# Block 0's Q moved behind its G, block 1 turned in squares on VectorE, seven-product Q on blocks 1 and 2: an adaLN linear-attention block

## The chip, the cores and the metric

The kernel runs on one core of one Trainium2 chip. The metric is the device time of one execution in microseconds (us), the median of several runs. TensorE is called PE here, VectorE DVE, ScalarE ACT, GpSimd POOL, and SyncE, which only issues DMAs, SP.

## What is computed

x is 2048 x 512, in float32; c is a conditioning vector of 512. The reference, cut to what matters:

```python
mod = (silu(c) @ w_mod).reshape(1, 6, 1, 512)        # sa, ca, ga, sb, cb, gb
h = layernorm(x) * (1 + ca) + sa
q, k, v = split of (h @ wqkv) into 32 heads of 16
pq, pk = phi(q), phi(k)                              # phi(t) = where(t > 0, t + 1, exp(t)) + 1e-6
kv  = einsum("bhsd,bhse->bhde", pk, v);  z = sum of pk over s
o   = einsum("bhqd,bhde->bhqe", pq, kv) / (einsum("bhqd,bhd->bhq", pq, z) + 1e-6)
x   = x + ga * (o @ wo)
h   = layernorm(x) * (1 + cb) + sb
x   = x + gb * (mish(h @ w1 + b1) @ w2)              # w1: 512 x 1792, w2: 1792 x 512
```

## The kernel before

The 2048 rows are four blocks of 512 rows (b = 0 to 3), and each block is four tiles of 128 rows (t) or, after it is turned, four tiles of 128 columns of D (j or k). Every product of float32 is made of three products of half-exact parts: `split` writes a tensor as a high part (a copy rounded to float32r, suffix h) and a low part (the rest, suffix l, by DVE), and `mm3` adds high x high, high x low and low x high on PE. So in front of each matmul group stand a copy on ACT or POOL and a subtraction on DVE.

The stages in the order of the program, as PE sees them:

- Modulation: `mod_col(i)` multiplies one 128-row piece of w_mod's transpose with silu(c) on DVE and sums it into a column of `mc`. The 24 columns come in groups of four; 0 to 7 are needed first, 8 to 11 are ga, 12 to 19 the second norm's, 20 to 23 gb. `mod_side` loads and makes them a few at a time beside other work.
- For each block: layer norm statistics and the apply (`ln_side`, `ln_begin`), turning the block so that D lies on the partitions, scale and shift by `mc` into `hf`, and `split` into `hT`. Blocks 0 and 1 are turned by PE (sixteen 128 x 128 transposes each; for block 1 in `transpose`, line 279). Blocks 2 and 3 are turned by DVE in 32 x 32 squares (`turn`, line 239), whose result sixteen DMAs of 64 KB carry to their places (`move_squares`, line 256: eight issued by SP, eight by POOL); ACT then reads them (`scale_turned`, line 270).
- K of the block (`k_unit`): products into PSUM, then `k_post`: two ACT passes (exp and relu), one DVE operation to `ku`, the split to `pk`; POOL adds `ku` into a running sum with an accumulating DMA. G of the block (`g_unit`): x's split normed rows times `pk`, added over all blocks in four PSUM banks `gacc`. kv is later made from G, without making V.
- The sums z of `pk` (`z_unit`, `z_side`), which scale the mask `hmask`.
- Q. For blocks 0 and 1 together with seven products of half size instead of eight (`q_sevens`, with sums of quarters prepared by `q_left` and `q_right`), for blocks 2 and 3 plainly (`q_unit`). `beside_q(n)` runs other work at seven places within. `phi` makes each Q tile in two ACT passes and one DVE operation.
- For each block `attend`: den, sixteen small products of Q with `hmask`, its reciprocal, a round trip through DRAM that spreads it over the partitions (`rden_d`, `rd`), Q times `rd`, and the split to `qs`. Then O (`o_unit`), Q times the product of kv and wo. Some O banks are seeded with x by an ACT copy ahead (`o_seed`, in the order of the list SEEDS), and an O tile's end is an ACT pass with a sum, further passes for the second norm (`norm_first`), and turns.
- The second half (w1, mish, w2), which takes the most time and which the change does not touch.

The order on each engine is the order in which the program emits its instructions, and each engine runs its queue in that order. Side work is a Python generator: `spawn` hands one over, and each `tick()` advances all by one `yield`. SBUF tiles come from 93 slots; PSUM from eight banks, four of tag `acc`, three `h`, one `tp`, each given to the next tile once all readers of the last are done.

`make_constants` (line 151 on) makes, on POOL, the constant `w32` and two masks of the block diagonal, `bmask` and `hmask`; DVE reduces `bmask` to `kvmask`. Before, it stands ahead of block 0's third G.

Of the kernel before, what the change touches and what calls it, by code (L numbers as in the profile page):

```python
# [10 lines left out]
AF = mybir.ActivationFunctionType  # L11
# [14 lines left out]
def block_kernel(ctx: ExitStack, tc: tile.TileContext, x, wqkv, wo, w1, b1t, w2, c, wmodt, out):  # L26
# [94 lines left out]
    for j in range(4):  # L121
        load_x(1, j)
    b1c = cst.tile([P, NF], F32, name="b1c")
# [150 lines left out]
    def transpose(key, b, j, sc0, sh0, ptag, hi_engine=act):  # L274

        if b < 2:
            p = ps(ptag, f"tp_{key}_{b}_{j}")
            for t in range(4):
                pe.transpose(p[:, P * t:P * (t + 1)], xt[key, b, t][:, P * j:P * (j + 1)], ident)

        def post():
            hf = sb(f"hf_{key}_{b}_{j}")
            if b < 2:
                hfx[b, j] = hf
                act.activation(hf, p, AF.Identity, bias=mc[:, sh0 + j:sh0 + j + 1],
                               scale=mc[:, sc0 + j:sc0 + j + 1])
            else:
                scale_turned(key, b, j, hf, sc0, sh0)
            yield from split(f"hT_{key}_{b}_{j}", hf, hT, (key, b, j), hi_engine=hi_engine)

        return post()
# [102 lines left out]
    def q_right(c):  # L394

        b11, b12, b21, b22 = [hfx.pop((b, k)) for k in (c, c + 2) for b in (0, 1)]
# [8 lines left out]
    def q_product(o, left, right, tag=None, onto=None):  # L405

        p = onto if onto is not None else ps(tag, f"pq_{left}_{o}")
        for c in range(2):
# [5 lines left out]
            mv_ = qb[right, c] if right[0] == "t" else hT["x", int(right[2]) - 1, c + 2 * (right[1] == "2")]  # L414
# [6 lines left out]
    def q_sevens(side):  # L421
# [21 lines left out]
        for o in range(2):  # L443
            q_product(o, "a12", "b21", onto=p11[o])
            result(0, o, p11[o], None)
# [8 lines left out]
        for o in range(2):  # L454
            result(0, 2 + o, q_product(o, "a22", "t4", onto=pa[o]), None)
        result(1, 2, pc[0], u3[0])
        side(4)
        pc[1] = q_product(1, "s1", "t1", "acc")
        result(1, 3, pc[1], u3[1])
        side(5)  # L460
        for o in range(2):
            q_product(o, "s4", "b22", onto=pc[o])
            result(1, o, pc[o], u2[o])
# [138 lines left out]
    for k in range(4):  # L602
        hi, lo = sb(f"hT_x_0_{k}h", F32R), sb(f"hT_x_0_{k}l", F32R)
        hT["x", 0, k] = hi, lo
        hf_k = hfx[0, k] = sb(f"hf_x_0_{k}")
# [125 lines left out]
    def z_side():  # L731
# [12 lines left out]
        yield  # L744
        for k in range(4):
# [952 lines left out]
```

## Time and profile before

| what | value |
|---|---|
| three runs | 477.77, 478.94, 479.31 us |
| their median | 478.94 us |
| span of the profiled execution | 476.5 us |
| PE busy | 470.8 us (99%) |
| DVE busy | 389.4 us (82%) |
| ACT busy | 312.0 us (65%) |
| POOL busy | 138.7 us (29%) |
| granted TensorE clock | 1.000 |

The span is the time from the first to the last instruction of the one execution that was profiled; the median of the runs is 2.4 us above it. Busy time counts an engine's instructions; register, branch and DMA-issuing instructions are not counted, except those that POOL issues. In a row of the order in time stand the start, the time that the row covers, the engine, the line, the operation, what is written and read, how many instructions, and in brackets the idle time ahead with what ended it. An instruction's time overlaps that of the next by a little, so the distance of two starts is what one costs on its queue.

### The profile page before, as it was taken

What the parts mean: (1) busy time and instruction counts of PE and PEld (TensorE: products, weight loads), DVE (VectorE), ACT (ScalarE), POOL (GpSimd) and SP (SyncE); (2) the same over time, 40 slices, a digit from 0 to 9 for tenths busy, and PEclk for the clock granted to TensorE, in tenths of its full rate; (3) what the DMA queues carried; (4) which work ended last, traced back from release to release, by engine and by line L of the source; (5) the groups of instructions that cost most, each with busy time, mean ns of one, the idle gap of its engine ahead of it and who ended that gap; (6) DMA issues with size and microseconds to landing.
All of it is one profiled execution on the core that took longest, in us unless ns stands there. A gap on an engine that the chain in (4) does not pass through costs nothing.

```text
span 476.5 us, 7242 instructions
## 1 busy us (share of the span) xinstructions
PE 470.8 (99%) x2354; PEld 387.6 (81%) x2354; DVE 389.4 (82%) x783; ACT 312.0 (65%) x566; POOL 138.7 (29%) x236
## 2 busy tenths in 40 slices
PE   8999999999999999999999999999999999999997
PEld 6778888878877888888888888888888888888887
DVE  6989898998998889697979863898544897779992
ACT  6976659756777976688688756694255676637700
POOL 3576261100023255012235325343011101354400
PEclk9999999999999999999999999999999999999999
DMA  8903649743685346936548669999633603498974
GB/s 302 383 22 74 126 93 268 187 144 105 229 213 147 115 119 184 319 119 196 178 153 243 201 187 324 366 308 261 202 96 89 132 2 89 110 221 163 239 157 106
DMA packets 81568, 85.44 MB, mean 179 GB/s; under 512 B 23505, under 2 KB 55769, under 8 KB 81530
## 3 DMA queue, kind: packets, MB, share of 16 engines
q1 hardware_dynamic: 55176, 47.08, 33.6%
q0 software_dynamic: 24096, 37.12, 29.6%
q10 hardware_dynamic: 2258, 0.79, 0.7%
q8 instruction: 18, 0.29, 0.2%
q14 instruction: 20, 0.16, 0.1%
HBM read 55.32 MB, written 22.81 MB: 164 GB/s over the span
## 4 chain that ended last, share of the span: by engine, by line
PE 93%; DVE 2%; ACT 2%; POOL 1%; DMA 1%; issue 0%; ACTq 0%
PE p_a L1265 15%; PE o L1004 9%; PE p_s L1265 8%; PE oacc L75 5%; PE oacc L74 5%; PE oacc L76 5%; PE m L74 5%; PE m L76 5%; PE m L75 5%; PE pk L319 5%; PE p L1265 4%; PE gacc L357 3%; PE gacc L359 2%; PE gacc L353 2%; PE pk L322 2%; PE pq_a L417 2%
## 5 line engine op out<-in xcount | busy, mean ns | idle before, releaser
L843 POOL DMA_DIRECT2D wb<-w2d x14 | 9.8, 705 | 65.1 <-PE p L1265 29.6
L1270 DVE TENSOR_TENSOR cb<-p_s,u 128x512 f32<-128x512 f32 x28 | 19.1, 685 | 11.8 <-ACT u L1319 10.2
L1257 ACT ACTIVATE ub<-cb,b1c 128x512 f32<-128x512 f32 x28 | 20.0, 719 | 9.4 <-DVE cb L1270 9.1
L199 POOL TENSOR_TENSOR rs_n<-rs_n,half 128x1 f32<-128x1 f32 x16 | 10.1, 630 | 38.8 <-DVE rs_n L225 18.7
L1594 POOL DMA_DIRECT2D wt_m<-w2t x20 | 14.0, 702 | 25.2 <-PE m L76 16.9
L1275 ACT ACTIVATE p<-p_a 128x512 f32<-128x512 f32 x12 | 7.0, 582 | 19.5 <-PE p_a L1265 11.7
L1319 ACT ACTIVATE u<-p_a 128x512 f32<-128x512 f32 x14 | 8.4, 597 | 13.6 <-PE p_a L1265 13.4
L1232 ACT ACTIVATE u<-p,b1c 128x512 f32<-128x512 f32 x14 | 9.6, 684 | 11.5 <-PE p L1265 11.5
L1232 ACT ACTIVATE u<-p_a,b1c 128x512 f32<-128x512 f32 x14 | 9.6, 686 | 8.5 <-PE p_a L1265 8.3
L849 POOL DMA_DIRECT2D w2b<-w2d x20 | 10.6, 541 | 12.9 <-PE oacc L76 6.8
L313 POOL DMA_DIRECT2D ku<-ku x10 | 8.9, 1036 | 18.5 <-DVE ku L304 18.3
L270 ACT ACTIVATE hf_n<-sq_n,mc 128x512 f32<-128x512 f32 x16 | 12.0, 802 | 2.4 <-DMA sq_n<-wide_n 2.4
L304 DVE SCALAR_TENSOR_TENSOR q<-e_q,relu_q 128x512 f32<-128x512 f32 x16 | 10.9, 687 | 1.6 <-ACT relu_q L302 1.6
L199 POOL TENSOR_TENSOR rs_x<-rs_x,half 128x1 f32<-128x1 f32 (+1 forms) x10 | 7.8, 785 | 13.8 <-DVE rs_x L194 13.0
L304 DVE SCALAR_TENSOR_TENSOR ku<-e_k,relu_k 128x512 f32<-128x512 f32 x16 | 10.9, 681 | 0.9 <-ACT relu_k L302 0.9
L190 DVE BATCH_NORM_STATS2 st_x<-x 128x6 f32<-128x512 f32 x13 | 8.8, 676 | 3.1 <-DMA x<-in_x_dram 3.1
L966 DVE SCALAR_TENSOR_TENSOR q<-q,rd 128x512 f32<-128x512 f32 x16 | 10.4, 684 | 1.2 <-DMA rd<-rden_d 1.2
L256 POOL DMA_DIRECT2D sq_n<-wide_n x16 | 8.7, 553 | 6.8 <-DMA rd<-rden_d 6.8
L175 DVE SCALAR_TENSOR_TENSOR wm<-wm,sc_row 128x512 f32<-128x512 f32 x16 | 10.5, 682 | 0.0
L256 POOL DMA_DIRECT2D sq_x<-wide_x x16 | 8.9, 566 | 5.1 <-DVE wide_x L239 4.6
L301 ACT ACTIVATE e_k<-pk 128x512 f32<-128x512 f32 x16 | 9.5, 591 | 1.4 <-PE pk L322 1.4
L208 ACT ACTIVATE x<-x,nb_x,rs_x 128x512 f32<-128x512 f32 x9 | 7.1, 809 | 4.8 <-DVE nb_x L203 3.9
(1638 smaller groups left out, 1857.1 us busy)
## 6 DMA issues: line engine op xcount, KB each, us to landing
wm<-in_wmodt_dram SPq DMA_DIRECT2D x24, 256.0 KB
w1p<-in_w_dram SPq DMA_DIRECT2D x24, 256.0 KB
w2b<-w2d POOLq DMA_DIRECT2D x20, 256.0 KB, 7.4
wt_m<-w2t POOLq DMA_DIRECT2D x20, 256.0 KB, 3.7
r<-in_x_dram SPq DMA_DIRECT2D x16, 256.0 KB
x<-in_x_dram SPq DMA_DIRECT2D x15, 256.0 KB
w2r<-in_w_dram SPq DMA_DIRECT2D x14, 256.0 KB
wb<-w2d POOLq DMA_DIRECT2D x14, 256.0 KB, 3.5
```

Source lines behind the costliest of these rows:

```text
L74: pe.matmul(o, st[0], mv[0], start=start, stop=False)
L75: pe.matmul(o, st[0], mv[1], start=False, stop=False)
L76: pe.matmul(o, st[1], mv[0], start=False, stop=stop)
L199: pool.tensor_tensor(y, y, half[:, lo:hi], op=ALU.pow)
L256: queues[n % len(queues)].dma_start(v[32 * m:32 * (m + 1), :, a, :], w[32 * a:32 * (a + 1), m:16:4].rearrange("p j t c -> p j (t c)"))
L304: dve.scalar_tensor_tensor(dst, e, 1.0, r, op0=ALU.min, op1=ALU.add)
L319: pe.matmul(p[t], hT["x", b, k][0][:, P * t:P * (t + 1)], wk[k][n], start=k == 0 and n == 0, stop=False)
L1004: pe.matmul(p, qs[b, g][l][:, ts], ms[g][r], start=not seeded and (g, l, r) == (0, 0, 0), stop=(g, l) == (3, 1), skip_group_check=seeded)
L1232: act.activation(u, p, AF.Mish, bias=b1c[:, f:f + 1])
L1257: act.activation(u, p, AF.Mish, bias=b1c[:, f:f + 1])
L1265: pe.matmul(p, st, mv, start=onto is None and c == 0 and i == 0, stop=c == 1 and i == 2, skip_group_check=onto is not None)
L1270: dve.tensor_tensor(out, p, u, op=ALU.add)
```

## The change

It leaves the products as they are, but for sixteen transposes, and moves work:

- Block 1 is turned as blocks 2 and 3 are: `transpose` becomes `normed`, without PE; four `turn` on DVE and one `move_squares` (eight DMAs from SP, eight from POOL) are added for it.
- Q of block 0 is made plainly, in two pairs of products (`q_pair`), right behind block 0's G. For that the Q weights are loaded early, ahead of x of blocks 2 and 3, and split early, half of the copies on POOL.
- `q_sevens` works on blocks 1 and 2 (MIDDLE), so `q_right` takes `hf` of these, and only block 3 has `q_unit`. All four O tiles of block 0 then follow Q of block 3 at once, and those of block 1 behind them.
- den of block 0 is made within `q_sevens`, den of the others earlier too; the last part of `z_side` moves up for it.
- `make_constants` moves behind the `ln_turn` of block 2.
- Columns 20 to 23 and 16 to 19 of the modulation move from `q_sevens` to the stretch behind block 1's K; columns 12 to 15 take their place.

```diff
@@ loads at the start
     for j in range(4):
         load_x(1, j)
+    for k in range(4):
+        load_wqkv(0, k)
+    for b in (2, 3):
+        for j in range(4):
+            load_x(b, j)
     b1c = cst.tile([P, NF], F32, name="b1c")
...
-    def transpose(key, b, j, sc0, sh0, ptag, hi_engine=act):
-
-        if b < 2:
-            p = ps(ptag, f"tp_{key}_{b}_{j}")
-            for t in range(4):
-                pe.transpose(p[:, P * t:P * (t + 1)], xt[key, b, t][:, P * j:P * (j + 1)], ident)
...
+    MIDDLE = 1, 2
+
+    def normed(key, b, j, sc0, sh0, hi_engine=act):
+
+        hf = sb(f"hf_{key}_{b}_{j}")
+        if b in MIDDLE:
+            hfx[b, j] = hf
+        scale_turned(key, b, j, hf, sc0, sh0)
+        yield from split(f"hT_{key}_{b}_{j}", hf, hT, (key, b, j), hi_engine=hi_engine)
...
@@ behind block 0's K
     step(kpost[3])
+    turn("x", 1, 0, xt["x", 1, 0])
     sums_shift("x", 1, 3, sums3)
     apply(1, 3, act, shift=False)
-    step(xsplit[3], kpost[3])
-    make_constants()
-    for b in (2, 3):
-        for j in range(4):
-            load_x(b, j)
+    wq_halves = [split(f"wq_{k}", wraw[0, k], wq, k, hi_engine=act if k % 2 else pool) for k in range(4)]
+    step(*wq_halves, xsplit[3], kpost[3])
+    for t in (1, 2, 3):
+        turn("x", 1, t, xt["x", 1, t])
+    move_squares("x", 1, (sp, pool))
+    for w in wq_halves:
+        run(w)
     g_unit(0, 2)
     spawn(ln_side(2))
     spawn(mod_side(range(8, 12), 2, 6))
     tick()
+    g_unit(0, 3)
+    tick()
+
+    def q_pair(b, two):
+
+        p = {g: ps("h", f"pq_{b}_{g}") for g in two}
+        for l, r in (0, 0), (0, 1), (1, 0):
+            for k in range(4):
+                for g in two:
+                    pe.matmul(p[g], wq[k][l][:, P * g:P * (g + 1)], hT["x", b, k][r],
+                              start=(l, r, k) == (0, 0, 0), stop=(l, r, k) == (1, 0, 3))
+        for g in two:
+            pq[b, g] = sb(f"q_{b}_{g}")
+            spawn(phi(p[g], f"q_{b}_{g}", pq[b, g]))
+
+    q_pair(0, (0, 1))
+    spawn(ln_begin(2))
+    tick()
     for j in range(4):
-        tr = transpose("x", 1, j, 4, 0, "h" if j < 3 else "tp", pool)
-        step(tr)
+        tr = normed("x", 1, j, 4, 0, pool if j % 2 else act)
+        next(tr)
         spawn(tr)
-    g_unit(0, 3)
-    spawn(ln_begin(2))
+    q_pair(0, (2, 3))
     spawn(ln_turn(2, (0, 1), ()))
     tick()
+    make_constants()
...
@@ blocks 1 to 3
         if b + 2 < NB:
             spawn(ln_side(b + 2))
+            spawn(mod_side([20, 21, 22, 23, 16, 17, 18, 19], 2))
...
-    SEEDS = [(0, 0), (0, 1), (0, 2), (0, 3), (), (), (1, 0), (1, 1), (), (), (), (2, 2)]
+    SEEDS = [(0, 0), (0, 1), (0, 2), (0, 3), (), (1, 0), (1, 1), (), (), (2, 2)]
...
@@ beside_q
+        if n == 2:
+            attending.append(attend(0, 3))
+            next(attending[0])
+            spawn(attending[0])
         if n == 4:
-            spawn(mod_side([20, 21, 22, 23, 16, 17, 18, 19], 2))
+            spawn(mod_side(range(12, 16), 1))
...
@@ behind q_sevens
     for g in range(4):
-        q_unit(2, g)
-        if g == 1:
-            spawn(attending)
+        if g == 3:
+            seed_next()
+        q_unit(3, g)
+        if g == 0:
+            spawn(attend(1, 4))
         if g == 2:
-            spawn(attend(1, 4))
-        if g == 1:
-            spawn(mod_side(range(12, 16), 1))
+            spawn(attend(2, 5, sp))
...
-    for g in range(4):
+    seed_next()
+    spawn_idle(early_rows[1])
+    for t in range(4):
         seed_next()
-        q_unit(3, g)
+        o_unit(0, t)
+        spawn(norm_first(0, t))
         tick()
...
```

Three places of the order that this makes. First POOL's queue behind its last cast for block 0 (`pk_0_3h`), before; `w32`, `bmask` and `hmask` are the constants, `hT_x_1_*` block 1's turned tiles:

```order
L84 CAST pk_0_3h_419<-ku_0_3_346 128x512
L153 MEMSET w32_139 128x128
L155 MEMSET bmask_427 128x128
L157 AFFINE_SELECT bmask_427<-bmask_427 128x128
L159 AFFINE_SELECT bmask_427<-bmask_427 128x128
L163 MEMSET hmask_140 128x128
```

and now, from the same cast on; `sq_x_1` and `sq_x_2` are the squares of blocks 1 and 2:

```order
L84 CAST pk_0_3h_443<-ku_0_3_370 128x512
L84 CAST wq_0h_450<-wr_0_0_111 128x512
L84 CAST wq_2h_456<-wr_0_2_115 128x512
L261 DMA sq_x_1_467<-wide_x_1_446 32x4x128 x8
L204 TENSOR_TENSOR rs_x_2_501<-rs_x_2_501,half_137 128x4
L84 CAST hT_x_1_1h_583<-hf_x_1_1_581 128x512
L84 CAST hT_x_1_3h_593<-hf_x_1_3_591 128x512
L261 DMA sq_x_2_645<-wide_x_2_640 32x4x128 x8
L158 MEMSET w32_163 128x128
L160 MEMSET bmask_663 128x128
L162 AFFINE_SELECT bmask_663<-bmask_663 128x128
L164 AFFINE_SELECT bmask_663<-bmask_663 128x128
```

The constants moved behind sixteen DMA issues, eight for each of the two blocks. Second, DVE's queue around the last turn of block 2 (`wide_x_2`), before; `ku_1_0` belongs to block 1's K:

```order
L239 STREAM_TRANSPOSE wide_x_2_549<-x_2_1_437 128x16x32
L304 SCALAR_TENSOR_TENSOR ku_1_0_587<-e_k_1_0_588,relu_k_1_0_589 128x512
L88 TENSOR_TENSOR xn_1_0l_593<-x_1_0_103,xn_1_0h_592 128x512
L90 SCALAR_TENSOR_TENSOR pk_1_0l_610<-ku_1_0_587,pk_1_0h_609 128x512
L304 SCALAR_TENSOR_TENSOR ku_1_1_613<-e_k_1_1_614,relu_k_1_1_615 128x512
```

and now; `wm_8` and `wm_9` are two `mod_col`:

```order
L244 STREAM_TRANSPOSE wide_x_2_640<-x_2_1_121 128x16x32
L166 TENSOR_REDUCE kvmask_165<-bmask_663 128x32
L300 SCALAR_TENSOR_TENSOR q_0_2_622<-e_q_0_2_630,relu_q_0_2_631 128x512
L300 SCALAR_TENSOR_TENSOR q_0_3_623<-e_q_0_3_634,relu_q_0_3_635 128x512
L300 SCALAR_TENSOR_TENSOR ku_1_0_689<-e_k_1_0_690,relu_k_1_0_691 128x512
L88 TENSOR_TENSOR xn_1_0l_695<-x_1_0_103,xn_1_0h_694 128x512
L180 SCALAR_TENSOR_TENSOR wm_8_509,mc_166<-wm_8_509,sc_row_167 128x512
L180 SCALAR_TENSOR_TENSOR wm_9_511,mc_166<-wm_9_511,sc_row_167 128x512
L90 SCALAR_TENSOR_TENSOR pk_1_0l_712<-ku_1_0_689,pk_1_0h_711 128x512
```

Between the turn and `ku_1_0` now stand the reduction of the mask, which stood far ahead, and two tiles of block 0's Q. Third, PE within `q_sevens`, where one of the seven products ends for the second column half and the next begins for the first; `pq_a11_1` and `pq_a11_0` are the banks of the two halves. Before:

```order
L417 MATMUL pq_a11_1_1313<-qt_0_1h_941,qs12_0l_1111 128x512
L417 MATMUL pq_a11_1_1313<-qt_1_1h_1019,qs12_1h_1169 128x512
L417 MATMUL pq_a11_1_1313<-qt_1_1l_1020,qs12_1h_1169 128x512
L417 MATMUL pq_a11_1_1313<-qt_1_1h_1019,qs12_1l_1170 128x512
L417 MATMUL pq_a11_0_1304<-qt_0_2h_978,qs34_0h_1127 128x512
L417 MATMUL pq_a11_0_1304<-qt_0_2l_979,qs34_0h_1127 128x512
```

and now, from the last two of the first product on:

```order
L413 MATMUL pq_a11_1_1424<-qt_1_1l_1145,qs12_1h_1296 128x512
L413 MATMUL pq_a11_1_1424<-qt_1_1h_1144,qs12_1l_1297 128x512
L959 MATMUL den_0_1500<-q_0_0_563,hmask_164 32x128 x4
L959 MATMUL den_0_1500<-q_0_1_564,hmask_164 32x128 x4
L959 MATMUL den_0_1500<-q_0_2_622,hmask_164 32x128 x4
L959 MATMUL den_0_1500<-q_0_3_623,hmask_164 32x128 x4
L413 MATMUL pq_a11_0_1415<-qt_0_2h_1103,qs34_0h_1254 128x512
```

The sixteen den products came in here from behind the last of the seven; on ACT the two `phi` passes on the bank that den takes (`pq_11_1`) stand behind two copies:

```order
L431 ACTIVATE qu2_1_1496<-pq_a11_1_1424 128x512
L82 ACTIVATE wos_0h_1520<-wo_0_1092 128x512
L297 ACTIVATE e_q_1_1_1524<-pq_11_1_1431 128x512
L298 ACTIVATE relu_q_1_1_1525<-pq_11_1_1431 128x512
L431 ACTIVATE qu3_0_1547<-pq_a11_0_1415 128x512
```

That order on ACT is the one of before; what moved is den.

More of the change, by code (lines that the diff above doesn't have):

```diff
@@ L444, in q_sevens @@
             q_product(o, "a12", "b21", onto=p11[o])
-            result(0, o, p11[o], None)
+            result(MIDDLE[0], o, p11[o], None)
             q_product(o, "s2", "t2", onto=pa[o])
@@ L743, in z_side @@
             dve.tensor_scalar(hmask[:, g, :], hmask[:, g, :], zc[:, g:g + 1], 1.0, op0=ALU.mult, op1=ALU.mult)
-        yield
-        for k in range(4):
-            zs[k] = sb(f"zs_{k}")
-            dve.tensor_scalar(zs[k], zbc, mc[:, k:k + 1], 1.0, op0=ALU.mult, op1=ALU.mult)
-        yield
-        yield
         dve.tensor_reduce(zh, zbc.rearrange("p (h r) -> p h r", r=16), op=ALU.add, axis=mybir.AxisListType.X)
@@ L756, in z_side @@
         dve.tensor_scalar(tiny_den, tiny_den, TINY, 1.0, op0=ALU.add, op1=ALU.mult)
+        yield
+        for k in range(4):
+            zs[k] = sb(f"zs_{k}")
+            dve.tensor_scalar(zs[k], zbc, mc[:, k:k + 1], 1.0, op0=ALU.mult, op1=ALU.mult)
     w2s, w2d, w2f, op_a = {}, {}, {}, {}
@@ L1153, in kv_side @@
                 yield
+    attending = []
     def beside_q(n):
```

42 lines of the change are left out of this document (8 added, 34 removed).

## The prediction

> **What bounds the kernel now.** I read the page first, then who TensorE (PE) waited for, then the busy time by stretches, and last the order in time of the engines that feed PE.
>
> ```profile
> span 476.5 us, 7242 instructions
> ...
> PE 470.8 (99%) x2354; PEld 387.6 (81%) x2354; DVE 389.4 (82%) x783; ACT 312.0 (65%) x566; POOL 138.7 (29%) x236
> ```
>
> PE is busy for 470.8 of 476.5 us. The list of its waits (waiting line, what released it, total us, times, longest) has five entries:
>
> ```profile
> PE warm L136 <- POOL ones L130: 1.1, 1, 1.1
> PE tp_x L279 <- ACT x L208: 0.4, 1, 0.4
> PE tp_late L565 <- ACT x L208: 0.4, 1, 0.4
> PE sc_bc L142 <- ACT c L140: 0.3, 1, 0.3
> PE tp_x L565 <- ACT x L208: 0.2, 1, 0.2
> ```
>
> The last of them in time is L279, just after 30 us. From there to the end PE never waits, so a product taken away is a gain of its full length, a product moved is worth nothing, and every new wait of PE is a loss of its full length. VectorE (DVE) is nearly full in the stretch in which the blocks' G and K products run; in the row below the columns are us of the stretch, then busy us of PE, weight load, DVE, ACT and POOL:
>
> ```profile
> 58.00:79.00 21.00, 21.00 (x95) 17.27 (x94) 19.95 (x34) 13.79 (x26) 9.11 (x14) 1.00 0.63 142
> ```
>
> DVE works 19.95 of 21 us there. It feeds PE with little to spare, so what the change gives DVE decides.
>
> **What goes.** The order in time on PE (start, us, engine, line):
>
> ```profile
> 30.41 0.49 PE L279 MATMUL tp_x<-ident,x 128*128 128x128 f32 x3
> ...
> 32.67 1.17 PE L353 MATMUL gacc<-pk_3h,xn_3h 128*128 128x512 f32 x4
> ...
> 46.64 1.07 PE L353 MATMUL gacc<-pk_0h,xn_0h 128*128 128x512 f32 x4
> 47.55 1.07 PE L357 MATMUL gacc<-pk_0h,xn_0l 128*128 128x512 f32 x4
> ...
> 78.53 1.07 PE L359 MATMUL gacc<-pk_3l,xn_3h 128*128 128x512 f32 x4
> ```
>
> The sixteen transposes with their wait take 32.67 - 30.41 = 2.26 us of PE. That is all that the change removes from PE. [...]
>
> Four matmuls take 47.55 - 46.64 = 0.91 us, so 0.227 each. The 48 of the first block's Q (10.9 us) only move: they now stand between block 0's G and block 1's K. A point of the program behind them stays on schedule if PE reaches it 10.9 us later than before.
>
> **What is moved: DVE waits behind GpSimd's DMA issues.** This is the main term. The masks (`make_constants`) are now made after block 2's `ln_turn`. On POOL they stand behind the eight square DMAs of block 2, which wait for DVE's last turn; on DVE the reduction `kvmask`, which waits for POOL's mask, stands right behind that turn, ahead of `ku` of block 1. I follow the queues, ACT first:
>
> ```profile
> 38.16 1.52 ACT L208 ACTIVATE x<-x,nb_x,rs_x 128x512 f32<-128x512 f32 x2 [3.74 <-DVE nb_x L203]
> 39.59 0.57 ACT L301 ACTIVATE e_k<-pk 128x512 f32<-128x512 f32 x1
> 40.07 0.58 ACT L302 ACTIVATE relu_k<-pk 128x512 f32<-128x512 f32 x1
> ...
> 52.12 0.82 ACT L270 ACTIVATE hf_x<-sq_x,mc 128x512 f32<-128x512 f32 x1 [1.68 <-DMA ku<-ku]
> 52.97 0.63 ACT L82 ACTIVATE hT_x_0h<-hf_x 128x512 fp32r<-128x512 f32 x1
> 53.50 0.80 ACT L270 ACTIVATE hf_x<-sq_x,mc 128x512 f32<-128x512 f32 x1
> ```
>
> G of block 0 ends at 32.67 + 12 x 0.227 - 2.26 = 33.1. The first two Q products take 24 x 0.227 = 5.4, to 38.6. ACT then does four passes of `phi` at 0.48 (to 40.7), the two applies of block 2 (1.5, to 42.3), and only then the four `hf` of block 1 (0.83 each) with two copies between (0.53): 46.7. A cast on POOL and the subtraction on DVE (about 0.7 each, as other cast and DVE rows here) end block 1's `hT` at 48.1. PE itself loses about 1.5 us up to here: the fourth Q product waits 1.0 for the bank that `relu` of the first frees (`h` has three), and K's last parts 0.5 for `hT`. Now DVE and POOL:
>
> ```profile
> 30.24 0.20 POOL L153 MEMSET w<- 128x128 f32 x1
> ...
> 41.76 4.56 POOL L256 DMA_DIRECT2D sq_x<-wide_x  x8 [4.63 <-DVE wide_x L239]
> ```
>
> ```profile
> 31.86 0.39 DVE L161 TENSOR_REDUCE kvmask<-bmask 128x32 f32<-128x128 f32 x1 [0.23 <-POOL bmask L159]
> ...
> 38.05 0.99 DVE L210 TENSOR_SCALAR x<-x,mv_x,rs_x 128x512 f32<-128x512 f32 x2
> 38.96 2.48 DVE L239 STREAM_TRANSPOSE wide_x<-x 128x512 f32<-128x512 f32 x4
> 41.37 0.65 DVE L304 SCALAR_TENSOR_TENSOR ku<-e_k,relu_k 128x512 f32<-128x512 f32 x1
> ...
> 47.26 0.68 DVE L175 SCALAR_TENSOR_TENSOR wm<-wm,sc_row 128x512 f32<-128x512 f32 x1
> 47.87 0.68 DVE L175 SCALAR_TENSOR_TENSOR wm<-wm,sc_row 128x512 f32<-128x512 f32 x1
> ...
> 76.95 0.68 DVE L90 SCALAR_TENSOR_TENSOR pk_3l<-ku,pk_3h 128x512 fp32r<-128x512 f32 x1
> ```
>
> From 48.1 DVE does two applies (0.9) and four turns (2.5): 51.5. POOL begins 0.3 later and issues for 4.56, then needs 31.86 - 30.24 = 1.6 for the mask: 58.0. DVE stands still for 6.5 us, then does the reduction (0.3) and two `q` (1.2), and begins `ku` of block 1 at 59.5, against 41.37 before: 18.1 later, where 10.9 was free. PE's G of block 1 needs that `ku` and a copy of it (0.6 + 0.7), so it starts at 60.8 and not at 46.64 + 10.9 = 57.5: already 3.3 us are lost.
>
> **What is added to DVE's full stretch.** Eight `mod_col` (columns 20 to 23 and 16 to 19) move from Q of the seven products to between here and block 2's G. Each is 47.87 - 47.26 = 0.61: 4.9 us. From `ku` to the last `pk_3l` of block 2 DVE took 76.95 - 41.37 = 35.6 us before, about 0.5 of it waits that the new work fills. So that `pk_3l` begins at 59.5 + 35.6 - 0.5 + 4.9 = 99.5 and ends at 100.2, and the last third of block 2's G cannot run before that: 100.2 instead of 78.53, 21.7 later, 10.9 of them free. **First term: +10.8 us, rounded to 11**, the 2.26 saved already in it (without it the whole chain starts later). Its ends: 3.3, if the eight fall into waits that I don't see; 13, if the squares of block 1 land late (below). Behind it DVE has 2.4 us less to do (the four `wq` halves are made early), but PE did not wait there before, so this returns nothing.
>
> **The den product of block 0.** It moves up between the second and third of the seven products, and takes bank `tp`, which p11 of the second column half holds until ACT has run `phi` on it. ACT's rows of that place before:
>
> ```profile
> 111.26 0.60 ACT L435 ACTIVATE qu<-pq_a 128x512 f32<-128x512 f32 x1 [1.15 <-PE pq_a L417]
> ...
> 112.75 0.60 ACT L302 ACTIVATE relu_q<-pq 128x512 f32<-128x512 f32 x1
> ```
>
> `qu` is taken when PE has finished the product ahead; PE would begin den at about 111.0, and `relu` ends at 113.35. **Second term: +2.4 us**, and nothing queued on PE can pass it. Its ends: 1.8 without the copy of wo between them, 3 if that copy waits for DVE.
>
> **O of blocks 0 and 1 back to back.** Before, Q of block 3 lay between and around them.
>
> ```profile
> 148.28 0.57 ACT L987 ACTIVATE r<-o 128x512 f32<-128x512 f32 x1
> 148.76 0.18 ACT L987 ACTIVATION_READ_ACCUMULATOR r<-o 128x1 f32 x1
> 148.97 0.73 ACT L1014 ACTIVATE scrap_n<-r,osum 128x512 f32<-128x512 f32 x1
> 149.61 0.18 ACT L1014 ACTIVATION_READ_ACCUMULATOR scrap_n<-r,osum 128x1 f32 x1
> 149.70 0.58 ACT L978 ACTIVATE o<-r 128x512 f32<-128x512 f32 x1
> ...
> 166.97 1.28 ACT L1226 ACT_TABLE_LOAD   x1
> ```
>
> Between the end of O's first tile and the seed of (1, 1) ACT has four `r` (0.69), four `scrap` (0.73), three seeds (0.52), four `qs` (0.53), two `n` (0.76) and the table load: 12.2 us. PE has four tiles in that time, 4 x 12 x 0.227 = 10.9. **Third term: +1.4 us**; 0 if ACT is ahead, 5 if `rd` comes late.
>
> **The rest at nothing.** The `wq` halves for the early Q: POOL is free at 30.24 and casts two by 31.5, ACT two by about 32.4, ahead of PE's 33.1; DVE's four subtractions behind the four turns of block 1 end near 36, and PE wants the first of them after sixteen matmuls, at 36.7. If one slips, PE loses what it slips, some 0.5. On SP four weight loads stand ahead of x of blocks 2 and 3, and the four of columns 8 to 11, which went in that stretch before, go behind block 1's squares: the same bytes, and DVE reads x of block 2 only near 36. The den products of blocks 1 and 2 move ahead of their use by over 8 us each and cost PE what they cost before. On POOL the `rden` round trips only move with them.
>
> **The sum.** 476.5 + 11 + 2.4 + 1.4 = 491.3 us of span; the runs' median of 478.94 is 2.4 above the profiled span, so **493.7 us**.
>
> **The rivals.**
> - *Saved and no more* (faster). If the reduction did not hold DVE, PE's 10.9 us of Q would let DVE, which gets four turns, four `wq` halves and four `q` (12 x 0.6 = 7.2 us), run ahead. 478.94 - 2.26 = 476.7. It decides where `ku` of block 1 begins: PE without waits would want G of block 1 at 46.64 + 10.9 - 2.26 = 55.3, so `ku` would have to begin by 54.0; I find 59.5. Chance 0.06.
> - *Only the hold counts*: the eight `mod_col`, den and O find cover. 478.94 + 3.3 = 482.2. The 0.3 to 0.6 us waits of DVE speak against it. Chance 0.10.
> - *More waits*: the sixteen squares of block 1 land after ACT wants them, and `rd` of block 1 takes as long as its longest here, so that the terms are 13, 2.4 and 5: 478.94 + 20.4 = 499.3. For it: ACT waited 1.68 us for the squares of block 2 in the row at 52.12. Chance 0.12.
> - *A slow restart of PE* after its pause of over 4 us at block 1's G. The first 18 small products of the program took 4.21 us, 0.234 each, the six later ones 0.83, 0.138 each:
>
> ```profile
> 1.10 4.21 PE L136 MATMUL warm<-ones 128*128 128x128 f32 x18 [1.10 <-POOL ones L130]
> ...
> 7.39 0.83 PE L136 MATMUL warm<-ones 128*128 128x128 f32 x6
> ```
>
>   Such a start costs 4.21 x (1 - 0.138 / 0.234) = 1.7 us: 495.4, if DVE's lateness does not hide it, which it mostly should. The granted clock stands at 1.00 throughout and shows nothing of it. [...] Chance 0.06.
>
> My forecast has the rest, 0.66. The range begins where the first term is at its low end and the others stay, 478.94 + 3.3 + 2.4 + 1.4 = 486.0, and ends at the third case: 486 to 499. It leaves out the first two cases. A difference of 0.3% is about what a measurement can tell from none. Faster is the first rival; 0.02 of the second lies so low that it is the same: faster 0.06, same 0.02, slower 0.92.
>
> **What would show it.** In the changed profile: no PE row for the transposes; a wait of DVE `kvmask` on POOL of about 6.5 us near 52 us; PE waits on `pk_h` of block 1 (over 3 us), on `hT` and `pk_l` in block 2, on `relu_q` ahead of den (2.4), and on a seed `o`. It is wrong if `kvmask` does not wait, if PE's total wait stays below 8 us, or if G of block 2 ends within 15 us of its old time.

## The result and the profile after

The changed kernel takes 516.41 us (median of four runs, 514.74 to 517.93), the kernel before 479.01: a ratio of 1.079 (95% interval 1.076 to 1.082), 37 us slower. The forecast was slower, 493.7 us, in a range that ends at 499. The profiled execution spans 515.5 us, 39.0 more than before. One profiled execution below, that of early_q_thin_2, was disturbed, so of that kernel only the times of the other executions are used.

The page of the changed kernel:

```profile
span 515.5 us, 7263 instructions
...
PE 479.5 (93%) x2338; PEld 388.1 (75%) x2338; DVE 392.8 (76%) x787; ACT 313.0 (61%) x566; POOL 144.1 (28%) x244
```

PE executes sixteen instructions fewer, the transposes, and yet is busy 8.7 us longer. The list of its waits (what waited, for whom, us in total, times, longest), where before all came to 2.4 us:

```profile
PE o L1016 <- ACT qs_0h L82: 13.0, 1, 13.0
PE gacc L349 <- ACT pk_0h L82: 4.1, 2, 3.5
PE o L1016 <- ACT o L990: 3.2, 3, 1.8
PE m_ps L74 <- ACT kv L1210: 2.4, 1, 2.4
PE den L959 <- issue: 2.2, 1, 2.2
...
PE gacc L355 <- DVE pk_0l L90: 1.1, 1, 1.1
...
PE m_ps L76 <- ACT kv L1210: 0.6, 1, 0.6
```

The first entry alone, for the first O tile of block 3, is nine times what the prediction allowed for all of the O stage.

Where the 39.0 us arise is read from two marks in PE's order: the first product with the sums of z (`zbc`, before and after; it comes behind the G of all blocks, ahead of the seven products) and O's first tile of block 3 (before at 185.29, after at 221.72):

```profile
102.42 0.62 PE L735 MATMUL zbc<-zsum,w 128*128 128x512 f32 x2
```

```profile
124.31 0.62 PE L752 MATMUL zbc<-zsum,w 128*128 128x512 f32 x2
...
160.79 0.47 PE L74 MATMUL m_ps<-wos_0h,kv 128*128 128x512 f32 x1 [2.39 <-ACT kv L1210]
...
221.72 0.80 PE L1016 MATMUL o<-m_0h,qs_0h 128*128 128x512 f32 x1 [12.99 <-ACT qs_0h L82]
```

Up to `zbc`: 124.31 - 102.42 - 10.88 (block 0's Q, which moved ahead of it) = 11.0 us lost. From there to O of block 3: 221.72 - 124.31 = 97.4 against 185.29 - 102.42 - 10.88 = 72.0, so 25.4 us lost. Behind it 2.6 more (515.5 - 221.72 against 476.5 - 185.29). The prediction had 11, and 2.4 + 1.4 = 3.8 for all that comes later.

**The first 11 us** look as forecast. DVE's `kvmask` stands behind block 2's last turn and waits for POOL, which first issues eight squares:

```profile
48.70 2.48 DVE L244 STREAM_TRANSPOSE wide_x<-x 128x512 f32<-128x512 f32 x4
57.09 0.37 DVE L166 TENSOR_REDUCE kvmask<-bmask 128x32 f32<-128x128 f32 x1 [5.90 <-POOL bmask L164]
```

```profile
51.48 4.38 POOL L261 DMA_DIRECT2D sq_x<-wide_x  x8 [4.33 <-DVE wide_x L244]
```

DVE stands still for 5.9 us (6.5 forecast), and block 2's G begins its last third at 100.19 (100.2 forecast).

**What was not forecast** is the hold of the squares of block 0 in the second norm. SP's queue, then who waits:

```profile
199.48 0.59 SPq L966 DMA_DIRECT2D rden_d<-rden  x1
202.02 2.56 SPq L970 DMA_DIRECT2D rd<-rden_d  x4
204.75 9.93 SPq L261 DMA_DIRECT2D sq_n<-wide_n  x8
```

```profile
216.82 0.71 DVE L244 STREAM_TRANSPOSE wide_n<-n 128x512 f32<-128x512 f32 x1 [12.76 <-DMA sq_n<-wide_n]
```

```profile
216.81 1.52 ACT L275 ACTIVATE hf_n<-sq_n,mc 128x512 f32<-128x512 f32 x2 [13.12 <-DMA sq_n<-wide_n]
...
221.05 0.61 ACT L82 ACTIVATE qs_0h<-q 128x512 fp32r<-128x512 f32 x1
```

`rden_d` and `rd` belong to block 3's `attend`, and they now stand ahead of block 0's eight squares on SP. The other eight squares wait on POOL for nothing of the kind, but ACT needs all sixteen, and DVE's next turn writes the one buffer that they read. ACT and DVE stop for 13 us, and Q of block 3 stands behind both. In the kernel before, the squares of block 0 were on SP ahead of that `rd` (issued at 165.93, `rden_d` of block 3 at 173.34), because two Q tiles of block 3 lay between O of block 0 and O of block 1. The eight issues themselves took 9.93 us here and 6.82 before; why, the runs don't show.

**The granted clock** was not 1.00 throughout. Columns: the stretch in us, its length, then PE, weight load, DVE, ACT and POOL busy (with the number of instructions), and the granted clock third from the end:

```profile
56.00:58.00 2.00, 0.58 (x3) 0.16 (x1) 0.91 (x2) 0.00 (x0) 1.72 (x7) 1.00 0.82 190
58.00:60.00 2.00, 0.00 (x0) 0.00 (x0) 2.00 (x5) 0.56 (x2) 0.56 (x2) 0.92 0.53 161
60.00:62.00 2.00, 1.88 (x5) 1.49 (x6) 2.00 (x7) 1.56 (x4) 0.67 (x1) 0.50 1.00 270
62.00:64.00 2.00, 2.00 (x8) 1.63 (x7) 2.00 (x5) 1.53 (x4) 0.87 (x1) 0.73 0.70 189
```

PE stopped at 56.6; some 3 us later (at 59.7) the clock was 0.50, and it came back (at 63.1) only after 3 us of work. The first eight matmuls of that G take 3.32 us (60.12 to 63.44) in place of 8 x 0.227 = 1.82. The same happens at `m_ps` (0.50 from 162.1 to 165.5), and behind the 13 us (from 213.3 to 226.9), where twelve matmuls take 227.19 - 221.72 = 5.47 in place of 2.72 (some 0.7 of that are short waits among them).

### The profile page after: what moved, and what is told of

Same layout as the page of the kernel before. It is cut to its first block, busy times and chain, and to the rows that moved or that the text cites. A ratio compares the mean times of both kernels' runs of the same rounds, so it can differ in the third digit from the quotient of the medians.

```text
span 515.5 us, 7263 instructions
## 1 busy us (share of the span) xinstructions
PE 479.5 (93%) x2338; PEld 388.1 (75%) x2338; DVE 392.8 (76%) x787; ACT 313.0 (61%) x566; POOL 144.1 (28%) x244
## 4 chain that ended last, share of the span: by engine, by line
PE 64%; DVE 14%; DMA 9%; ACT 5%; issue 4%; POOL 2%; SPq 1%; DVEq 0%; ACTq 0%; POOLq 0%
PE p_a L1273 14%; PE p_s L1273 7%; PE oacc L76 5%; PE oacc L75 5%; PE oacc L74 5%; PE m L75 4%; PE m L74 4%; PE m L76 4%; PE p L1273 4%; PE o L1016 3%; DMA rd<-rden_d 3%; DMA w1p<-in_w_dram 2%; DVE wm L180 2%; DVE wide_x L244 1%; PE pk L315 1%
## 5 line engine op out<-in xcount | busy, mean ns | idle before, releaser
L1278 DVE TENSOR_TENSOR cb<-p_s,u 128x512 f32<-128x512 f32 x28 | 19.2, 687 | 12.2 <-ACT u L1327 10.6
L1016 PE MATMUL o<-m_0h,qs_0h 128*128 128x512 f32 x16 | 7.2, 448 | 16.5 <-ACT qs_0h L82 13.0
L261 POOL DMA_DIRECT2D sq_x<-wide_x x24 | 13.4, 570 | 15.1 <-issue 9.2
L1016 PEld LDWEIGHTS o<-m_0h,qs_0h 128*128 128x128 f32 x16 | 3.1, 193 | 19.2 <-ACT qs_0h L82 13.4
L244 DVE STREAM_TRANSPOSE wide_n<-n 128x512 f32<-128x512 f32 x8 | 5.6, 708 | 13.0 <-DMA sq_n<-wide_n 12.8
L966 POOL DMA_DIRECT2D rden_d<-rden x2 | 1.4, 724 | 46.1 <-DVE rden L964 46.1
L300 DVE SCALAR_TENSOR_TENSOR q<-e_q,relu_q 128x512 f32<-128x512 f32 x16 | 10.9, 696 | 1.1 <-ACT relu_q L298 1.1
L1008 POOL DMA_DIRECT2D x1d<-r x8 | 4.4, 553 | 25.8 <-DVE r L1003 25.8
```

What stands on the lines that cost most here:

```text
L261: queues[n % len(queues)].dma_start(v[32 * m:32 * (m + 1), :, a, :], w[32 * a:32 * (a + 1), m:16:4].rearrange("p j t c -> p j (t c)"))
L300: dve.scalar_tensor_tensor(dst, e, 1.0, r, op0=ALU.min, op1=ALU.add)
L1016: pe.matmul(p, qs[b, g][l][:, ts], ms[g][r], start=not seeded and (g, l, r) == (0, 0, 0), stop=(g, l) == (3, 1), skip_group_check=seeded)
L1278: dve.tensor_tensor(out, p, u, op=ALU.add)
```

## The experiments

All are compared with the kernel before on the same chip; the changed kernel's 516.4 us are the base of the first group. The kernel before took 479.0 us beside the changed kernel and 478.1 to 478.8 beside the others, so a difference of under 1 us between groups says nothing.

**1. The masks back ahead of block 0's third G.** 

```diff
     step(*wq_halves, xsplit[3], kpost[3])
+    make_constants()
...
-    make_constants()
```

> The changed kernel (span 515.5 us) with make_constants back ahead of block 0's third G, nothing else. Theory: DVE's kvmask no longer stands behind GpSimd's eight square DMAs of block 2, so DVE and all behind it in block 1 come up to 6.5 us earlier; TensorE's wait of 3.5 us at block 1's G and the 1.5 us by which its first eight matmuls there ran long go, and block 2's G ends 5 to 6.5 us earlier: time 5 to 6.5 us below the changed kernel's, span 509 to 510.5. Rival: the eight columns of the modulation that now lie in block 1's stretch of DVE hold block 2 alone, and the pause only hides them: not over 1.5 us lower, span 514 or more, and the waits of TensorE move on into block 2.

Measured 510.5 us (ratio 1.068, 1.065 to 1.071), 5.9 below the changed kernel. The first theory holds: PE begins block 1's G without a wait, at 58.47, and is at `zbc` 4.5 us earlier, at 119.78. The masks are not free at that place either: `kvmask` waits 1.6 us for POOL there, and K of block 1 ends 1.9 us later than in the changed kernel.

**2. Den of block 0 back behind the seven products.** 

```diff
-        if n == 2:
-            attending.append(attend(0, 3))
-            next(attending[0])
-            spawn(attending[0])
...
     kvs = {}
+    attending.append(attend(0, 2))
+    next(attending[0])
```

> The changed kernel with den of block 0 back behind the seven products, its second half one step later, nothing else. Theory A (the bank alone): TensorE's 2.2 us wait within the seven products goes, span 513 (2.4 lower). Theory B (the bank and the queues): with den made early, block 0's Q times rd and its splits stand on DVE and ACT ahead of kvc and kv, so kv comes late; with den back, TensorE's 3.0 us wait for kv and the 2.5 us by which its twelve matmuls there run long go too: 6 to 8 us lower, span 507.5 to 509.5.

Measured 512.4 us, 4.0 lower: between the two. The wait for the bank and those for kv went, but PE now waits 2.7 us at block 3's first Q tile (the profile names no cause; see the end of experiment 6), and the granted clock is 0.50 from about 149 to 155 us.

**3. Den of block 3 four tiles earlier.** 

```diff
         spawn(norm_first(0, t))
+        if t == 1:
+            spawn(attend(3, 7, sp))
...
-            if n == 5:
-                spawn(attend(3, 3, sp))
```

> The changed kernel with den of block 3 started behind block 0's second O tile, four tiles earlier, its use left where it was, nothing else. Theory: SyncE's eight square DMAs of block 0 stood behind rden and rd of block 3, and rden of block 3 behind DVE's late work; DVE and ACT then both waited for these squares (12.8 and 13.1 us) ahead of Q of block 3, and TensorE 13.0 us for O of block 3. Now rd of block 3 is done before the squares come: TensorE's wait there falls below 3 us, the 2.7 us by which the first twelve matmuls behind it run long go as well, 12 to 16 us lower, span 500 to 504. Rival: the squares are late by themselves (DVE's last turn of block 0 was late, and the sixteen transfers take their 12 us from one buffer): TensorE's wait stays above 8 us, span 509 or more.

Measured 506.2 us (1.058, 1.055 to 1.061), 10.3 lower: less than the 12 to 16 expected, and the most of any single edit. SP's queue in this kernel, and what is left of PE's wait:

```profile
182.14 0.58 SPq L966 DMA_DIRECT2D rden_d<-rden  x1
187.58 2.56 SPq L970 DMA_DIRECT2D rd<-rden_d  x4
196.50 5.26 SPq L261 DMA_DIRECT2D sq_n<-wide_n  x8
```

```profile
PE o L1016 <- ACT qs_0h L82: 2.7, 1, 2.7
```

The squares go as soon as DVE's last turn is done, and 13.0 us of wait became 2.7. That most of the wait was SP's order, and not the turns or the transfers themselves, is shown. A part (ACT and DVE still wait 4.8 and 4.6 us for the squares) belongs to the rival.

**4. The loads of w1's second group ahead of `rden` of block 2 on SP**, as they stood before:

```diff
+        if g == 1:
+            load_w1(1)
         if g == 2:
             spawn(attend(2, 5, sp))
```

> The changed kernel with the two loads of w1's second group (w1p) put ahead of rden and rd of block 2 on SyncE, as they stood before, nothing else. Theory: DVE's 5.4 us wait for w1p near 183 us goes, and the last turn of block 0 and rden of block 3 come as much earlier; TensorE's wait of 13.0 us for O of block 3 falls to 7 to 8: 5 to 6 us lower, span 509.5 to 510.5. Rival: DVE's wait only moves on to rd of block 2 or to ACT's results, since ACT sets the pace of the O tiles there: not over 1.5 us lower.

Measured 513.5 us, 2.9 lower, between the two. PE's wait for O of block 3 fell from 13.0 to 9.4 us.

**5. Several at once.** masks_and_columns is the edit of experiment 1 and this:

```diff
             spawn(ln_side(b + 2))
-            spawn(mod_side([20, 21, 22, 23, 16, 17, 18, 19], 2))
...
         if n == 4:
-            spawn(mod_side(range(12, 16), 1))
+            spawn(mod_side([20, 21, 22, 23, 16, 17, 18, 19], 2))
...
+        if g == 1:
+            spawn(mod_side(range(12, 16), 1))
```

four_undone is the edits of experiments 1 to 4, and four_and_columns has the lines above as well.

> The changed kernel with make_constants early (as in masks_early, 510.5 us) and, besides, columns 20 to 23 and 16 to 19 of the modulation back in the seven products and 12 to 15 back behind them. Theory: the eight columns are 4.9 us of DVE in the stretch of blocks 1 and 2, where DVE still feeds TensorE late; with them away block 2's G ends 2 to 5 us earlier: 505.5 to 508.5 us. Rival: with the masks early DVE has caught up before block 2's G, so that the columns lie in its waits: within 1 us of masks_early, 509.5 to 511.5.

> The four edits of masks_early, den0_back, den3_early and w1_early at once. If they are separate places, their gains of 5.9, 4.0, 10.3 and 2.9 us add up to 23.1: 493.3 us. The last two act on the same wait of TensorE for O of block 3, so w1_early's 2.9 should not count again in full: 493 to 496. Rival: all of them only move one bound, ACT's and DVE's chain from kv to O, from place to place: 500 or more.

> four_undone with the eight columns of the modulation moved back as well. What stays of the change is block 0's Q behind its G, block 1's squares, seven products on blocks 1 and 2, and O of blocks 0 and 1 back to back. Theory: what the columns are worth in masks_and_columns comes off here too, 2 to 5 us below four_undone. The removed transposes would then be seen only if under 476.7 us is reached, which I don't expect, since O back to back (a wait of 1.7 us for its first seed and 1.5 for later ones) and the late squares of block 1 stay: 487 to 492. Rival: what stays of the change costs nothing by itself: 477 to 480.

Measured 512.7, 499.8 (1.045, 1.043 to 1.047) and 496.7 us (1.039, 1.037 to 1.040). The columns do what the sum said: PE is at `zbc` at 115.39 with them away and at 119.78 with the masks alone, 4.4 us for eight `mod_col`:

```profile
115.39 0.62 PE L752 MATMUL zbc<-zsum,w 128*128 128x512 f32 x2
```

But the time of the whole did not fall at all for it (512.7 against 510.5, outside what both theory and rival said). What is gained ahead of the seven products is lost again behind them, in waits at block 3's first Q tile (5.3 us, none in masks_early) and for O's seeds (6.5, 3.2 in masks_early). In the same way the four edits give 16.7 us together, not the 20 to 23 expected, and with the columns away too 19.7, where 24 to 29 were expected. Something behind the seven products other than PE's work sets the time.

**6. What that bound is.** Three variants of four_and_columns. den0_later starts den of block 0 at place 3 of `beside_q`; kv_early adds to it, with the lines of kv's product and copies in two functions:

```diff
-        if n == 2:
+        if n == 3:
             attending.append(attend(0, 3))
...
         tick()
+        if n == 4:
+            kv_product()
+        if n == 5:
+            kv_copies()
```

> four_and_columns (496.7 us), but den of block 0 stands neither behind the seven products nor where the change put it: behind the third product (place 3 of beside_q in place of 2), where ACT has long read the bank that den takes. Theory: TensorE then waits for no bank (2.2 us in the changed kernel), and Q of block 0 times rd and its splits are done before the splits of m, so DVE no longer waits 2.4 us for rd ahead of them; of TensorE's 6.8 us wait for the first O seed some 3 us go, and with the wait the 2.3 us by which the twelve matmuls behind it run long shrink: 491 to 494. Rival: Q times rd stands ahead of kvc again, as in the changed kernel, and kv is late: 496 or more.

> den0_later with the product kv, its mask, split and copies moved from behind the seven products to their places 4 and 5, about 7 us of TensorE earlier. Theory of the lost cover: what the change took away between kv and the first O tile is the 10.9 us of Q that now run ahead of block 1's K; before, 8 Q tiles stood between kv and the end of O's second tile, now 4. Starting kv 7 us earlier gives most of that back: 3 to 7 us below den0_later, TensorE's wait for the first O seed under 2 us. Rival: the first O seed waits for rd and the phi passes of block 3's Q, not for kv: within 1 us of den0_later.

> four_and_columns with 24 further matmuls (5.4 us of TensorE, into a bank that nobody reads) between block 3's Q and the first O tile, where TensorE stood 6.8 us waiting for a seed and then ran its next twelve matmuls 2.3 us long at a granted clock of 0.5. They leave the computation as it is and add work only. Theory: the gap is a lack of cover, so the work is free, and since TensorE no longer pauses as long, the granted clock stays at 1.00 there: 1.5 to 3 us faster than four_and_columns, 494 to 495. Rival 1: the clock has nothing to do with the pause: same time, 496.7. Rival 2: the gap is not a pause for others but TensorE's own queue: 5.4 slower, 502.

The filler, in short:

```diff
+    fill = ps("h", "fill")
+    for i in range(24):
+        pe.matmul(fill, wq[i % 4][0][:, 0:P], hT["x", 3, i % 4][0], start=i == 0, stop=i == 23)
     seed_next()
     spawn_idle(early_rows[1])
```

Measured: den0_later 500.5 us, the time that the rival gave. Q times `rd` does stand ahead of kvc again, which runs at 148.0 us, against 138.9 in four_and_columns; but PE never waits for kv in this kernel, and its wait for the first seed fell from 6.8 to 3.1 us, as the theory had it. What grew is the wait at block 3's first Q tile, from 0.8 to 4.0 us. kv_early 495.8, 4.7 below den0_later and within what the theory said, but that wait of 4.0 us is gone in it too, so the 4.7 don't show that cover came back; the wait for the first seed fell to 1.6, and there are 4.2 us at den of block 2 and 4.2 at block 1's first seed. filled_gap 495.5: 5.4 us more of PE's work cost nothing. The windows of four_and_columns, then of filled_gap, over the same place:

```profile
154.00:161.00 7.00, 0.71 (x4) 0.25 (x2) 6.93 (x15) 4.27 (x9) 2.36 (x4) 0.92 0.44 124
161.00:166.00 5.00, 4.46 (x11) 3.50 (x12) 4.66 (x10) 2.49 (x5) 0.00 (x0) 0.50 0.47 102
```

```profile
154.00:161.00 7.00, 6.87 (x31) 5.35 (x29) 6.93 (x16) 4.25 (x9) 2.37 (x4) 1.00 0.45 131
161.00:166.00 5.00, 4.44 (x20) 3.54 (x21) 4.68 (x10) 3.73 (x9) 0.55 (x1) 1.00 0.39 103
```

DVE is at 6.93 of 7 us in both. With the pause filled the granted clock stays at 1.00, and 20 matmuls go through in the next 5 us in place of 11. The medians (495.5 and 496.7) are too near each other, with one run of filled_gap above, to put a size on that gain; that the work was free is plain.

The wait at block 3's first Q tile is no wait for data. In masks_and_columns it falls in the middle of a tile, ahead of a product whose two operands PE has read before:

```profile
141.61 0.40 PE L75 MATMUL pq<-hT_x_0l,wq_0h 128*128 128x512 f32 x1
147.31 0.80 PE L76 MATMUL pq<-hT_x_0h,wq_0l 128*128 128x512 f32 x1 [5.31 <-issue]
```

The six kernels that have it (den0_back, masks_and_columns, four_undone, four_and_columns, den0_later, filled_gap) have it at the same place of PE's order, behind the 1472nd or 1473rd recorded matmul or weight load, where the 128 small products of kv have just gone by, and it ends 1.3 to 1.6 us after a 16 KB transfer of kind `instruction` has landed (here at 145.90). In the ten other kernels (early_q_thin_2 left out) that transfer had landed 2.6 us or more before PE came to the same count (in the changed kernel 5.0 us: 145.00 and 149.96), and PE doesn't wait there. That PE waited for this transfer is the author's reading of these times; no run varied it. The wait is 5.3 us of masks_and_columns, 4.0 of den0_later, 2.7 of den0_back, 1.9 of four_undone, 1.8 of filled_gap and 0.8 of four_and_columns, and the first three of these can't be read as if only the moved work differed.

**7. Columns elsewhere.** columns_late is kv_early with this, and columns_in_block1 is kv_early without the lines of experiment 5:

```diff
-            spawn(mod_side([20, 21, 22, 23, 16, 17, 18, 19], 2))
+            spawn(mod_side([20, 21, 22, 23], 2))
...
-            spawn(mod_side(range(12, 16), 1))
...
     seed_next()
+    spawn(mod_side([16, 17, 18, 19, 12, 13, 14, 15], 2))
     spawn_idle(early_rows[1])
```

> kv_early (495.8 us) with columns 12 to 19 of the modulation moved on from the stretch of the seven products and block 3's Q to behind it, beside O of block 0, where DVE is idle half of the time. Theory: in kv_early TensorE waited 4.2 us at den of block 2 for DVE, which had eight columns (4.9 us) among its work there, then 1.6 us for the first O seed, and ran 2 us long behind these pauses at a granted clock of about 0.5; most of that goes: 488 to 491. Rival: ACT's phi passes, not DVE's columns, hold den and the seed: within 1 us of kv_early.

> kv_early with the eight columns left where the change put them, in block 1's stretch (so the masks, den of block 0, den of block 3, w1p and kv are moved, the columns are not). By the rows of masks_early and masks_and_columns TensorE comes to the sum of z 4.4 us later for it (119.8 against 115.4 us), and behind that DVE has 4.9 us less to do. If the stretch behind the seven products is bound by DVE, the two cancel: 494 to 497. If it is bound by TensorE, the 4.4 us stay: 499 to 501.

Measured 501.3 and 495.3 us. columns_late came out slower, and its theory was not put to the test: the wait at den of block 2 stayed at 4.2 us because the columns moved were not those ahead of it. Four `mod_col` (columns 20 to 23) still stand on DVE in front of `rden` of block 1, whose bank den of block 2 takes, and DVE works there without a wait:

```profile
148.05 0.69 DVE L180 SCALAR_TENSOR_TENSOR wm<-wm,sc_row 128x512 f32<-128x512 f32 x1
...
151.69 0.69 DVE L180 SCALAR_TENSOR_TENSOR wm<-wm,sc_row 128x512 f32<-128x512 f32 x1
...
152.31 1.89 DVE L300 SCALAR_TENSOR_TENSOR q<-e_q,relu_q 128x512 f32<-128x512 f32 x3
154.11 0.34 DVE L962 TENSOR_SCALAR rden<-den,tiny_den 128x128 f32<-128x128 f32 x1
```

Whether ACT's passes would hold den without them is open. The loads of the moved columns, behind block 2's `rd` on SP, held DVE (2.2 and 1.3 us for `wm`) within the O tiles. In columns_in_block1 PE is at `zbc` 4.4 us later than in kv_early (119.84 and 115.5), and the time is the same (495.3 and 495.8): the 4.4 us cancel, as with a stretch that PE does not bound. Neither kernel has the wait without a named cause at block 3's first Q tile.

**8. Is Q cover, or work?** The last three ask that on both sides of the move. before_thin_q leaves out the low parts of block 2's Q, eight products of twelve (the edit below); early_q_thin_2 does the same to block 0's Q, in `q_pair` of columns_in_block1; early_q_thin is columns_in_block1 once more.

```diff
+            if b == 2:
+                pe.matmul(p, wq[k][0][:, gs], hT["x", b, k][0], start=k == 0, stop=k == 3)
+                continue
             mm3(p, [w[:, gs] for w in wq[k]], hT["x", b, k], k == 0, k == 3)
```

> The kernel before, with only the four high-by-high products of the twelve in each Q tile of block 2 (the low parts are left out): 32 matmuls of 0.227, 7.3 us of TensorE, fewer between kv and O. If TensorE is the bound there, as its busy time of 99% says, the time falls by all of it: 471.6 us. Theory of the lost cover: these products hide the chain from kv over m, den, rd and the split of Q to the first O tile, which DVE ends only about when TensorE wants it (the last split of block 0's Q begins at 146.3 us, its use at about 147); then TensorE gets waits in place of the products, and the time falls by 2 us at most, or rises if the pauses bring the granted clock down: 476 to 480.

> columns_in_block1 once more, as the base of the next one: 494.5 to 497.

> columns_in_block1 (495.3 us) with only the four high-by-high products of the twelve in each Q tile of block 0 (the low parts are left out): 32 matmuls, 7.3 us of TensorE, fewer ahead of block 1's K. If TensorE is the bound there, the time falls by all of it, to 488. Theory: DVE and ACT set the pace from block 1's squares to block 2's G, so TensorE comes to the sum of z only 0 to 2.5 us earlier (119.8 us in the base) and waits in between: 493 to 495.5.

The kernel before, with 7.3 us of PE's work taken out at the place from which the change took Q away, takes 479.4 us against 478.2 (1.0023, 1.0010 to 1.0036): no faster, if anything slower. In the kernel before the last split of block 0's Q ends at 147.02, 0.2 us before PE takes it:

```profile
146.34 0.68 DVE L88 TENSOR_TENSOR qs_3l<-q,qs_3h 128x512 fp32r<-128x512 f32 x1
```

```profile
147.21 0.40 PE L1004 MATMUL o<-m_3h,qs_3l 128*128 128x512 f32 x1
```

The waits of PE in before_thin_q in this part of the program, where the kernel before has none:

```profile
PE gb_ps L476 <- DVE rden L954: 2.0, 1, 2.0
PE m_ps L74 <- ACT kv L1199: 1.3, 1, 1.3
...
PE m_ps L76 <- ACT kv L1199: 0.6, 1, 0.6
...
PE o L1007 <- DVE qs_2l L88: 0.4, 1, 0.4
```

O begins at 144.48 us, with all the products at 144.71; counted from `zbc` (103.04 and 102.42) that is 0.9 us sooner for 7.3 us less work. A part of the rest is the clock, 0.50 from 140.05 to 143.46, in which 9 matmuls ran in place of 15 (3.41 / 0.227). At the new place the same 7.3 us are worth as little: early_q_thin_2 takes 495.1 us, its base, run once more, 495.4. Q ran beside DVE and ACT at the old place, with no room to spare. That it runs beside their work at the new place too is not shown by this: 4.4 us gained ahead of `zbc` were lost again behind it in experiment 7, and so might these be.

## Why the prediction was wrong

**Right: the main term.** +11.0 us at `zbc`, 11 forecast, and by the two causes named: the hold of `kvmask` 4.5 us (experiment 1, net of what the early masks cost there), the eight columns 4.4 (experiment 5; 4.9 forecast), and 2.1 for the small waits less the transposes saved. DVE's hold of 5.9 us was to reach PE in full; the 4.5 hold some 1.5 us of slow clock that the sum had at nothing. That the last third of block 2's G agrees to 0.01 us is luck: it was to wait for `pk_3l`, which ended at 99.64, while PE's last wait ahead of it was for `pk_3h`, 0.35 us.

**Right: den of block 0.** PE ends the product ahead at 132.96 and starts den at 135.34, 2.4 us, as forecast, with `relu_q`, which frees the bank, ending at 135.24. But only the bank was priced. What follows den on DVE and ACT (Q times `rd`, its splits) moved too, ahead of kvc and kv, and PE waited 3.0 us for kv at `m_ps` and ran on at a granted clock of 0.50 (162.1 to 165.5). den0_back gave 4.0 us, and not 2.4, with a new wait of 2.7 in it.

**Wrong: "a product moved is worth nothing", and with it what stands behind `zbc`.** The step took the 99% of PE's page for a bound all along: "From there to the end PE never waits, so a product taken away is a gain of its full length, a product moved is worth nothing". before_thin_q shows the contrary for the stretch from kv to O: products taken away there gain nothing, since the chain over kv, m, den, `rd` and the split of Q ends just when PE wants it. The rows at 146.34 and 147.21 show as much: PE does not wait when others are just in time. The change took 10.9 us of such cover away. For all behind `zbc` the sum had 3.8 us, and the runs show 28.0 (25.4 and 2.6): 2.4 for den, 3.0 of waits for kv, 3.5 for seeds and O's `r`, 13.0 for Q of block 3, and 1.9 and 2.8 for the matmuls that ran long behind two of these pauses; 1.4 are not placed. The third term itself, ACT's chain beside the O tiles, is the 3.5 for seeds and `r`: more than the 1.4 (12.2 - 10.9 is 1.3) and within its end of 5. What failed is the rest, which the prediction put at nothing.

**Wrong: SP's queue.** "On POOL the `rden` round trips only move with them" was said of POOL, and SP was followed only up to block 1's squares. SP carries `rd` of blocks 2 and 3, w1p and half of the squares; with Q no longer between O of blocks 0 and 1 their order turned round, which the order of the program would have shown. den3_early puts this at 10.3 us, the largest single piece, and w1_early at 2.9, both on the same wait. None of the three signs of being wrong came: `kvmask` waited, PE's waits came to far over 8 us, and block 2's G was late; not one of them looks at the stretch behind `zbc`.

**The rivals.** The slow restart of PE had the chance 0.06, one place and 1.7 us. There were three places, and about 1.5, 1.9 and 2.8 us by their rows (3.32 for 1.82; twelve at `m_ps` in 165.81 + 0.23 - 160.79 - 0.60 = 4.65 for 2.72; 5.47 for 2.72), 6.2 in all. It is less a rival than a surcharge on waits: here the matmuls behind the pauses of 3.5, 2.4 and 13.0 us ran 1.5, 1.9 and 2.8 us long. In the trace the granted clock was at 0.50 some 3 us after the stop at 56.6, a pause of 3.5 us, and also behind the pause of 2.4 us at `m_ps` (from 162.1). Of *more waits*, the squares of block 1 came in time: ACT takes the first at 42.23 without a wait.

**What stays open.** The best versions (columns_in_block1 495.3, filled_gap 495.5, kv_early 495.8) are 17 us above the kernel before. That this is cover lost behind the seven products is shown in kind by before_thin_q and filled_gap, but not summed wait by wait; 6.5 us of it lie ahead of that stretch (in columns_in_block1 `zbc` comes at 119.84, and 102.42 + 10.88 = 113.30 would be on schedule). No version that beats the kernel before was found.

## What to carry to other kernels

An engine at 99% is no proof that it is the bound in each stage: before work is moved away from a place, take it out there in a trial, or find out how late the result comes that it is waiting beside; if that comes just in time, the work is cover, and moving it can cost up to its length. When stages close up, follow each DMA queue to the end of the program: a round trip that waits for a late engine, in front of transfers that others need, cost 10.3 us here, more than any other single piece. On top of its waits, the changed kernel's matmuls ran 1.5, 1.9 and 2.8 us long behind the pauses of 3.5, 2.4 and 13.0 us. And before an edit is read as a test, look in its trace whether the instructions that were to move are the ones that stood in the way.

## What the runs showed of the hardware

In the changed kernel the granted clock fell to 0.50 only 3 to 5 us after TensorE had stopped (at 59.7 for the stop at 56.6, at 162.1 for that at 158.4, at 213.3 for that at 208.7), and it stayed there for 3 to 5 us of the work that follows (to 63.1, 165.5 and 226.9).

Not every pause has such a stretch behind it. Den of block 0 waited 2.2 us in the changed kernel and in masks_early: in the changed kernel (133.12 to 135.34) the clock stayed at 1.00, in masks_early it was 0.50 from 130.60 to 134.01. columns_in_block1 and early_q_thin are one program: the profiled execution of the first waited 3.2 us at den of block 2 and has a mean granted clock of 1.000, that of the second has 0.996. What decides it the runs don't show, and none varied it.

The changed kernel's times scatter by more (514.74 to 517.93) than those of the kernel before (477.77 to 479.31); why, wasn't tried.
